# Retention into a snake feed-forward, one core: who transposes q and k of chunks five to eight, and in which slots the later transposes are issued

## The chip, the cores and the metric

The kernel runs on one core of a Trainium2 chip. The metric is the device time of one execution in microseconds (us). The engines are called TensorE (PE in the profile, with PEld for its weight loads), VectorE (DVE), ScalarE (ACT), GpSimd (POOL) and SyncE (SP). SyncE and GpSimd issue the DMA transfers of this kernel.

## What is computed

Two layers in a row. The first is a recurrent retention over 4 batches, 8 heads, 768 positions and head width 64; the second is a feed-forward layer on the 3072 resulting rows of width 512, with a hidden width of 2048 and the activation h + sin(alpha h)^2 / alpha.

```python
for t in range(S):
    state = gamma[None, :, None, None] * state + np.einsum('bhd,bhe->bhde', k[:, :, t], v[:, :, t])
    y[:, :, t] = scale * np.einsum('bhd,bhde->bhe', q[:, :, t], state)
...
h = x @ w_in
s = np.sin(alpha * h)
g = h + s * s / (alpha + 1e-09)
return (g @ w_out).astype(np.float32)
```

## The kernel before

The sequence of each batch is cut into six chunks of 128 positions, 24 chunks in all. The list `order` (also called `P`) first has the first chunk of each of the four batches, then the other five chunks of batch 0, of batch 1, and so on. So P[0] to P[3] are the first chunks, and P[4] to P[8] are the rest of batch 0. The feed-forward layer works on groups of 4, 2, 4, 4, 4, 4 and 2 chunks (`sizes`, L49).

**Loading.** `load_chunk` (L73) brings q, k and v of a chunk by three DMAs from GpSimd's queue, which also change float32 to bfloat16. q and k lie side by side in one tile `qkr`, v in `vr`. GpSimd multiplies v of later chunks by a decay table in place (`scale_v`, L111), between the loads that it issues (L429 to L435); VectorE does it for P[0], P[4] and P[5].

**One chunk of the retention** takes these steps:

- The transposed q and k of all heads are put into `qkT` (128 x 8 x 128, six buffers). There are three ways: `half_T` (L177) for the first three chunks; `stage_T` (L190), eight transposes by TensorE into the PSUM tile `pt` and one copy by VectorE (L197); and `turn` (L199), one DMA from SyncE that transposes from `qkr` into `qkT`.
- `stage_A` (L204): eight matmuls from `qkT` into `pa`, and VectorE's multiplication by the causal mask into `aT` (L214).
- `stage_M` (L233): eight matmuls of the state `s_bd` with `qkT`, eight of `aT` with v, both into `py`; VectorE writes `xT`, the input of the feed-forward layer (L255). It also adds the chunk to the state (`stage_S`, L217), which ScalarE copies to `s_bd` (`keep_S`, L228).

The tiles `pt` of stage_T and `py` of stage_M share one PSUM buffer (tag `ty`).

**The feed-forward layer.** `ff_in(g, f, ...)` makes one of 16 blocks of the hidden layer for a group: four matmuls into `ph` (L270), sine and square on ScalarE (L272, L274), and one VectorE instruction into `gT` (L277). `ff_out` (L284) is one of 16 matmuls that add up one chunk's output in `po` (L287); after the sixteenth, ScalarE copies it to one of three `o_sb` tiles and SyncE stores it. `ph` and `po` share four PSUM buffers.

**The order** is written out by hand; each engine and each queue works through its own instructions in that order. After the first batch of chunks, phase 0 does the rest of group 0's blocks. Then comes a stretch, here called the front (L437 to L451): `outs` is a list of 50 output matmuls of group 0, `fill(n)` issues the next n of them, and between the fills stand the stages of P[4] and P[5]. Phase 1 (L452) does the 16 blocks ("slots") of group 1, P[4] and P[5], whose moving operand has 256 columns, spreads the remaining 19 output matmuls over them, and attaches the stages of P[6] to P[9] to slots through a dictionary. From phase 2 on, slots have 512 columns, and the stages of the next group's chunks and the `turn` of the chunk two further on are attached by a formula (L455 to L470).

Before the change, the DMA transposes of P[4] to P[7] are issued together at L437, ahead of the front; those of P[8] to P[11] in slots 2, 6, 10 and 14 of phase 1.

Of the kernel before, what the change touches and what calls it, by code (L numbers as in the profile page):

```python
# [15 lines left out]
def kernel(  # L16
# [94 lines left out]
    def scale_v(j, eng):  # L111
        eng.tensor_mul(raw["v", j], raw["v", j], kg[:, j % NCH, :, None].to_broadcast([128, H, D]))  # L112
# [77 lines left out]
    def stage_T(j):  # L190
        pt = psum.tile([128, 2 * NP, 128], BF16, name="pt", tag="ty")
        st["qkT", j] = work.tile([128, 2 * NP, 128], BF16, name="qkT", tag="qkT", bufs=6)
        for i in range(2):
            for p in range(NP):
                nc.tensor.transpose(pt[:, i * NP + p, :],
                                    raw["qk"[i], j][:, 2 * p:2 * p + 2, :].rearrange("p h d -> p (h d)"), ident)
        nc.vector.tensor_copy(st["qkT", j], pt)  # L197

    def turn(j):  # L199

        st["qkT", j] = work.tile([128, 2 * NP, 128], BF16, name="qkT", tag="qkT", bufs=6)
        nc.sync.dma_start_transpose(out=st["qkT", j], in_=raw["qk", j].rearrange("p i h d -> p (i h d)"))

    def stage_A(j):  # L204
        qkT = st["qkT", j]
        pa = psum.tile([128, 2, NP, 128], F32, name="pa", tag="pa")
        for p in range(NP):
            for e in range(2):
                r = slice(64 * e, 64 * e + 64)
                nc.tensor.matmul(pa[:, e, p, :], qkT[r, NP + p, :], qkT[r, p, :],  # L210
                                 start=(p == 0), stop=True, skip_group_check=True)
        aT = work.tile([128, 2, NP, 128], BF16, name="aT", tag="aT", bufs=2)
        m = dec.rearrange("p e n t -> p (e n) t") if j % NCH == 0 else mask_bc
        nc.vector.tensor_mul(aT.rearrange("p e n t -> p (e n) t"), pa.rearrange("p e n t -> p (e n) t"), m)  # L214
        st["aT", j] = aT

    def stage_S(j):  # L217
        c = j % NCH
        if c == 0:
            st["ps"] = psum.tile([128, NP, D], F32, name="ps", tag="ps")  # L220
        ps = st["ps"]
        for p in range(NP):
            for e in range(2):
                nc.tensor.matmul(ps[64 * e:64 * e + 64, p, :], raw["k", j][:, 2 * p + e, :], raw["v", j][:, 2 * p + e, :],  # L224
                                 start=(c == 0 and p == 0), stop=True, skip_group_check=True)
        return ps

    def keep_S(j, ps):  # L228
        for e in range(2):
            r = slice(64 * e, 64 * e + 64)  # L230
            nc.scalar.copy(s_bd[(j % NCH + 1) % 2][r, :, r], ps[r, :, :])  # L231

    def stage_M(j):  # L233
        c = j % NCH
        g, i = place[j]
        if g not in xT:
            xT[g] = work.tile([128, KS, sizes[g] * C], BF16, name="xT", tag="xT", bufs=3)
        qkT, aT, vs = st["qkT", j], st["aT", j], raw["v", j]
        py = psum.tile([128, NP, 128], F32, name="py", tag="ty")
        if c > 0:  # L240
            for p in range(NP):
                for e in range(2):
                    r = slice(64 * e, 64 * e + 64)
                    nc.tensor.matmul(py[r, p, :], s_bd[c % 2][:, p, r], qkT[:, p, :],  # L244
                                     start=(p == 0), stop=True, skip_group_check=True)
        for p in range(NP):
            for e in range(2):
                nc.tensor.matmul(py[64 * e:64 * e + 64, p, :], vs[:, 2 * p + e, :], aT[:, e, p, :],  # L248
                                 start=(c == 0 and p == 0), stop=True, skip_group_check=True)
        x = xT[g][:, :, i * C:(i + 1) * C]  # L250
        if c == 0:
            nc.scalar.copy(x, py)
            return
        ps = stage_S(j) if c < NCH - 1 else None
        nc.vector.tensor_mul(x, py, qg[:, c])  # L255
        if ps is not None:
            keep_S(j, ps)
# [42 lines left out]
    def out_pieces(g, tss):  # L300
        return [lambda ts=ts, f=f: ff_out(g, ts, f) for ts in tss for f in range(FF)]
# [55 lines left out]
    def phase(g, outs, att, squares, slots=range(FF)):  # L357

        no, n0, done = len(outs), len(slots), 0
        for n, f in enumerate(slots):  # L360
            add = ff_in(g, f, squares[f % len(squares)])
            for fn in att.get(f, ()):
                fn()
            add()
            while done < no * (n + 1) // n0:
                outs[done]()
                done += 1

    def T(j):
        return lambda: turn(j)  # L370

    def A(j):
        return lambda: stage_A(j)

    def M(j):
        return lambda: stage_M(j)
# [7 lines left out]
    def SK(j):  # L384
        return lambda: keep_S(j, stage_S(j))
# [33 lines left out]
    P = order  # L419
# [4 lines left out]
    def fill(n):  # L424
        for _ in range(n):
            outs.pop(0)()
# [7 lines left out]
        if n in (13, 15, 17):  # L434
            scale_v(order[(n - 11) // 2], nc.gpsimd)  # L435

    for j in P[4:8]:  # L437
        turn(j)
    fill(7)
    scale_v(P[4], nc.vector)  # L440
    fill(5)
    stage_A(P[4])
    keep_S(P[0], stage_S(P[0]))
    fill(5)
    scale_v(P[5], nc.vector)
    fill(5)
    stage_A(P[5])
# [2 lines left out]
    stage_M(P[5])  # L450
    fill(3)  # L451
    phase(1, outs,  # L452
          {1: [A(P[6])], 2: [T(P[8])], 5: [A(P[7]), M(P[6])], 6: [T(P[9])],
           9: [A(P[8]), M(P[7])], 10: [T(P[10])], 13: [A(P[9]), M(P[8]), SK(P[9] - 1)], 14: [T(P[11])], 15: [M(P[9])]}, "A")
    for g in range(2, NG):  # L455
        att = {}
        if g + 1 < NG:
            js = groups[g + 1]
            for i, j in enumerate(js):
                a = i * FF // len(js)  # L460
                n = P.index(j) + 2
                if n < NJ:
                    att.setdefault(a + 2, []).append(T(P[n]))
                att.setdefault(a + 1, []).append(A(j))
                if i > 0:
                    att[a + 1].append(M(js[i - 1]))
                if j % NCH == 1:
                    att[a + 1].append(SK(j - 1))
            att.setdefault(FF - 2, []).append(M(js[-1]))
        phase(g, out_pieces(g - 1, range(sizes[g - 1])), att, "A")  # L470
# [32 lines left out]
```

## Time and profile before

| | us |
|---|---|
| median of three runs (lowest, highest) | 227.9 (227.52, 228.04) |
| the profiled execution | 228.16 |
| its span, first to last instruction | 226.1 |
| TensorE busy | 211.4 |
| ScalarE busy | 164.8 |
| VectorE busy | 130.0 |
| GpSimd busy | 90.3 |

The time of the profiled execution includes 2.06 us outside the span. TensorE is the busiest engine, and busy time is not time at full speed: it counts a matmul at half clock as twice as long. The page's row of the granted clock has 40 slices of 5.65 us. It is at full speed in all but one, the ninth, which begins at 45.2 us. The DMA engines are busy until about 130 us, while the chunks are loaded, and nearly idle after that. The table of DMA issues gives a median of 8.8 us from issue to landing for the 20 transposes, and 9.5 to 10.5 us for the loads of q, k and v.

### The profile page before, as it was taken

Reading aid. Unit: us, or ns where it says so; the run is one execution under the profiler, and the core shown is the slowest. Engines: PE = TensorE matmul, PEld = TensorE weight load, DVE = VectorE, ACT = ScalarE, POOL = GpSimd, SP = SyncE. Lnnn points to the kernel's source line nnn. Section 1 sums busy time; section 2 is a strip of 40 time slices with the busy share of each in tenths; the row PEclk is TensorE's granted clock in tenths of the full one; section 3 lists DMA queues with packets and bytes.
Section 4 is the critical chain, followed back from the end, with each engine's and each line's share of the span. In section 5 each row is a group of like instructions: output and inputs, shape, how many; then the busy total and the mean of one; then the engine's idle time right before and its main releaser. Section 6 shows DMA issues by size and latency. Waiting matters only on the chain.

```text
span 226.1 us, 4226 instructions
## 1 busy us (share of the span) xinstructions
PE 211.4 (93%) x1629; PEld 106.3 (47%) x1629; DVE 130.0 (58%) x214; ACT 164.8 (73%) x322; POOL 90.3 (40%) x105
## 2 busy tenths in 40 slices
PE   7998889579898999999999999999999999999993
PEld 3544433135566454544544544554544454556541
DVE  4777798434787576775645745664753364433300
ACT  7678768223998899978787787687778868777720
POOL 8965346668499788789962000000000000000000
PEclk9999999959999999999999999999999999999999
DMA  9999999999999999999995421431211011111112
GB/s 132 148 185 193 207 204 158 136 152 160 183 183 123 142 172 126 182 156 174 184 169 84 96 65 27 97 96 37 58 46 46 8 42 46 46 49 46 48 60 79
DMA packets 103732, 25.71 MB, mean 114 GB/s; under 512 B 96528, under 2 KB 100640, under 8 KB 103712
## 3 DMA queue, kind: packets, MB, share of 16 engines
q0 software_dynamic: 77024, 13.37, 84.1%
q1 hardware_dynamic: 26688, 12.07, 27.5%
q8 instruction: 12, 0.20, 0.4%
q14 instruction: 8, 0.07, 0.1%
HBM read 27.27 MB, written 6.29 MB: 148 GB/s over the span
## 4 chain that ended last, share of the span: by engine, by line
PE 70%; DMA 15%; POOL 5%; DVE 3%; ACT 3%; issue 2%; POOLq 0%; SPq 0%
PE po L287 34%; PE ph L270 28%; DMA qkr<-in_k_dram 7%; DMA w_in<-in_moe_w_in_dram 4%; DMA qkT<-qkr 4%; PE pa L210 3%; PE py L244 2%; POOL qkr L83 2%; DVE aT L214 2%; PE py L248 2%; ACT s L272 1%; POOL vr L83 1%; PE ps L224 1%; ACT s L274 1%; DVE xT L255 1%
## 5 line engine op out<-in xcount | busy, mean ns | idle before, releaser
L277 DVE SCALAR_TENSOR_TENSOR gT<-s,rec_alpha,ph 128x512 bf16<-128x512 f32 (+3 forms) x118 | 75.7, 645 | 69.8 <-ACT s L274 69.1
L287 PE MATMUL po<-w_out,gT 128*128 128x512 bf16 x384 | 103.6, 386 | 1.9 <-DVE gT L277 1.3
L270 PE MATMUL ph<-xT,w_in 128*128 128x512 bf16 (+3 forms) x472 | 101.5, 339 | 1.3 <-DVE gT L277 0.7
L272 ACT ACTIVATE s<-ph,alpha_sb 128x512 f32<-128x512 f32 (+3 forms) x118 | 71.4, 606 | 31.9 <-PE ph L270 31.8
L270 PEld LDWEIGHTS <-w_in 128*128 128x128 bf16 x472 | 45.3, 98 | 47.5 <-issue 5.0
L274 ACT ACTIVATE s<-s 128x512 f32<-128x512 f32 (+3 forms) x109 | 60.3, 553 | 3.5
L287 PEld LDWEIGHTS <-gT 128*128 128x128 bf16 x384 | 35.9, 99 | 40.0 <-DVE gT L277 4.0
L214 DVE TENSOR_TENSOR aT<-pa,mask 128x1024 bf16<-128x1024 f32 x20 | 24.4, 1221 | 7.8 <-PE pa L210 7.8
L112 POOL TENSOR_TENSOR vr<-vr,kg 128x512 bf16<-128x512 bf16 x21 | 22.1, 1057 | 16.1 <-DMA vr<-in_v_dram 16.1
L83 POOL DMA_DIRECT2D vr<-in_v_dram x24 | 21.8, 906 | 3.2 <-DMA w_in<-in_moe_w_in_dram 1.6
L83 POOL DMA_DIRECT2D qkr<-in_q_dram x23 | 21.3, 925 | 3.8 <-DMA w_in<-in_moe_w_in_dram 1.7
L83 POOL DMA_DIRECT2D qkr<-in_k_dram x23 | 20.4, 888 | 3.8 <-DMA w_out<-in_moe_w_out_dram 3.4
L231 ACT CAST s_bd<-ps 64x256 bf16<-64x256 f32 x40 | 14.4, 361 | 9.1 <-PE ps L224 8.7
L297 ACT COPY o_sb<-po 128x512 f32<-128x512 f32 x23 | 13.2, 574 | 6.9 <-PE po L287 6.9
L255 DVE TENSOR_TENSOR xT<-py,qg 128x512 bf16<-128x512 f32 x20 | 13.7, 683 | 2.3 <-PE py L248 2.2
L210 PE MATMUL pa<-qkT 64*128 64x128 bf16 x192 | 9.7, 222 | 4.4 <-DMA qkT<-qkr 4.2
L309 PE MATMUL spare<-warm 128*128 128x512 bf16 x36 | 12.5, 462 | 1.2 <-DVE warm L131 1.2
L210 PEld LDWEIGHTS <-qkT 64*128 64x128 bf16 x192 | 5.5, 95 | 13.5 <-issue 7.5
L248 PE MATMUL py<-aT,vr 128*64 128x128 bf16 x192 | 9.5, 219 | 0.5 <-DVE rec_alpha L347 0.2
L244 PE MATMUL py<-qkT,s_bd 128*64 128x128 bf16 x160 | 8.3, 225 | 0.2 <-DVE xT L255 0.2
L248 PEld LDWEIGHTS <-vr 128*64 128x64 bf16 x192 | 6.9, 110 | 1.5 <-issue 1.1
L244 PEld LDWEIGHTS <-s_bd 128*64 128x64 bf16 x160 | 5.2, 109 | 4.0 <-issue 1.9
(58 smaller groups left out, 64.0 us busy)
## 6 DMA issues: line engine op xcount, KB each, us to landing
out_dram<-o_sb SPq DMA_DIRECT2D x24, 256.0 KB, 2.3
vr<-in_v_dram POOLq DMA_DIRECT2D x24, 128.0 KB, 10.5
qkr<-in_q_dram POOLq DMA_DIRECT2D x23, 128.0 KB, 9.5
qkr<-in_k_dram POOLq DMA_DIRECT2D x23, 128.0 KB, 10.4
w_in<-in_moe_w_in_dram POOLq DMA_DIRECT2D x4, 512.0 KB, 11.1
w_out<-in_moe_w_out_dram POOLq DMA_DIRECT2D x4, 512.0 KB, 14.9
qkT<-qkr SPq DMA_TRANSPOSE x20, 8.8
q<-in_q_dram SPq DMA_DIRECT2D x1, 256.0 KB, 3.5
```

Source lines behind the costliest of these rows:

```text
L83: nc.gpsimd.dma_start(out=t, in_=chunk_of(src, j))
L112: eng.tensor_mul(raw["v", j], raw["v", j], kg[:, j % NCH, :, None].to_broadcast([128, H, D]))
L210: nc.tensor.matmul(pa[:, e, p, :], qkT[r, NP + p, :], qkT[r, p, :], start=(p == 0), stop=True, skip_group_check=True)
L214: nc.vector.tensor_mul(aT.rearrange("p e n t -> p (e n) t"), pa.rearrange("p e n t -> p (e n) t"), m)
L244: nc.tensor.matmul(py[r, p, :], s_bd[c % 2][:, p, r], qkT[:, p, :], start=(p == 0), stop=True, skip_group_check=True)
L248: nc.tensor.matmul(py[64 * e:64 * e + 64, p, :], vs[:, 2 * p + e, :], aT[:, e, p, :], start=(c == 0 and p == 0), stop=True, skip_group_che ...
L255: nc.vector.tensor_mul(x, py, qg[:, c])
L270: nc.tensor.matmul(ph, w_in[:, i, f * 128:(f + 1) * 128], xT[g][:, i, lo:hi], start=(i == 0), stop=(i == KS - 1))
L272: nc.scalar.activation(out=s, in_=ph, func=ACTF.Sin, scale=alpha_sb[:, f:f + 1])
L274: nc.scalar.activation(out=s, in_=s, func=ACTF.Square)
L277: return lambda: nc.vector.scalar_tensor_tensor(gT[g][:, f, lo:hi], s, rec_alpha[:, f:f + 1], ph, op0=ALU.mult, op1=ALU.add)
L287: nc.tensor.matmul(po[g, ts], gT[g][:, f, ts * C:(ts + 1) * C], w_out[:, f, :], start=(f == 0), stop=(f == FF - 1))
```

## The change

q and k of P[4] to P[7] are transposed by `stage_T` instead of `turn`: for P[4] and P[5] between the fills of the front, for P[6] and P[7] in slots 0 and 3 of phase 1. The DMA transposes of P[8] to P[11] are issued in slots 0, 4, 8 and 12. The other attached stages of phase 1 move too: stage A of P[6] from slot 1 to 2, of P[7] (with stage M of P[6]) from 5 to 6, of P[8] (with stage M of P[7]) from 9 to 10. Slots 13 and 15 and all later phases keep their order.

```diff
     def T(j):
+        return lambda: stage_T(j)
+
+    def X(j):
         return lambda: turn(j)
...
-    for j in P[4:8]:
-        turn(j)
     fill(7)
+    stage_T(P[4])
     scale_v(P[4], nc.vector)
     fill(5)
     stage_A(P[4])
     keep_S(P[0], stage_S(P[0]))
     fill(5)
+    stage_T(P[5])
     scale_v(P[5], nc.vector)
     fill(5)
     stage_A(P[5])
...
     phase(1, outs,
-          {1: [A(P[6])], 2: [T(P[8])], 5: [A(P[7]), M(P[6])], 6: [T(P[9])],
-           9: [A(P[8]), M(P[7])], 10: [T(P[10])], 13: [A(P[9]), M(P[8]), SK(P[9] - 1)], 14: [T(P[11])], 15: [M(P[9])]}, "A")
+          {0: [T(P[6]), X(P[8])], 2: [A(P[6])], 3: [T(P[7])], 4: [X(P[9])], 6: [A(P[7]), M(P[6])], 8: [X(P[10])],
+           10: [A(P[8]), M(P[7])], 12: [X(P[11])], 13: [A(P[9]), M(P[8]), SK(P[9] - 1)], 15: [M(P[9])]}, "A")
...
-                    att.setdefault(a + 2, []).append(T(P[n]))
+                    att.setdefault(a + 2, []).append(X(P[n]))
```

## The prediction

> **What bounds the kernel now.** I read the page first, then the chain of work that ended last, then TensorE's own timeline at the place that the chain names, and last the clock in windows of 1 us. Chunks are named by their place in the kernel's order: P[4] to P[7] are chunks five to eight. "T" is a transpose by TensorE (stage_T), "X" one by the DMA (turn), "A" and "M" are stage_A and stage_M, "SK" is a state update.
>
> The page's first line, and two neighbouring pieces of the chain (start, duration, what):
>
> ```profile
> span 226.1 us, 4226 instructions
> ```
>
> ```profile
> 21.08 16.43 DMA qkr<-in_k_dram
> 37.60 9.12 DMA qkT<-qkr
> ```
>
> P[4]'s k has landed at 37.51, and its X, issued at 37.60, lands at 46.72. TensorE's timeline shows who waits (start, duration, line, instruction, count; in brackets the idle time and what ended it):
>
> ```profile
> 41.98 0.60 PE L287 MATMUL po<-w_out,gT 128*128 128x512 bf16 x2 [0.15 <-DVE gT L277]
> 46.77 0.61 PE L210 MATMUL pa<-qkT 64*128 64x128 bf16 x8 [4.18 <-DMA qkT<-qkr]
> 47.30 0.43 PE L224 MATMUL ps<-vr,kb 128*64 128x64 bf16 x8
> 47.66 4.16 PE L287 MATMUL po<-w_out,gT 128*128 128x512 bf16 x10
> 51.76 0.40 PE L210 MATMUL pa<-qkT 64*128 64x128 bf16 x8
> 52.08 0.41 PE L244 MATMUL py<-qkT,s_bd 128*64 128x128 bf16 x8
> ```
>
> Stage A of P[4] waits 4.18 us for that X, and afterwards ten po matmuls take 4.16 us, over 0.4 us each. The clock says why (window, its length, busy time of PE, PEld, DVE, ACT, POOL; then the granted clock, the DMA share, GB/s):
>
> ```profile
> 43.40:44.40 1.00, 0.00 (x0) 0.00 (x0) 0.00 (x0) 0.00 (x0) 0.07 (x1) 1.00 3.50 120
> 44.40:45.40 1.00, 0.00 (x0) 0.00 (x0) 0.00 (x0) 0.00 (x0) 0.00 (x0) 0.59 3.56 130
> ...
> 50.40:51.40 1.00, 1.00 (x4) 0.30 (x2) 0.00 (x0) 0.59 (x1) 0.00 (x0) 0.50 1.80 157
> 51.40:52.40 1.00, 1.00 (x22) 0.55 (x22) 0.20 (x1) 0.00 (x0) 0.76 (x1) 1.00 2.41 151
> ```
>
> A mean of 0.59 in a window that starts at 1.00 and ends at 0.50 puts the fall near 44.6, some 2.2 us after TensorE ran dry. The clock is back at 51.4. So one late transpose costs twice: the wait, and 4.6 us of matmuls at half speed.
>
> **The change part by part.** The profiled execution took 228.16 us, 2.06 more than its span; the runs' median of 227.9 is 0.26 below it.
>
> *The wait and the slow clock go.* At full speed a 512-column matmul takes 0.216 us (the 41.98 row: 0.60 for two, of which 0.38 is one matmul's own latency). TensorE could issue stage A at 41.98 + 2 x 0.216 = 42.41, and did at 46.77: 4.36 us. From there to 51.76 it needed 4.99 us for eight pa, eight ps and ten po; at full speed 0.32 (51.76 to 52.08), about 0.23 and 2.16, together 2.71. That is 2.28 us more. Gain 6.64.
>
> *What T costs instead.* The first batch's last chunk was transposed by stage_T already:
>
> ```profile
> 18.75 0.40 PE L195 MATMUL pt<-ident,qkr 128*128 128x128 bf16 x4 [0.18 <-DMA qkr<-in_q_dram]
> ...
> 20.01 0.69 DVE L197 COPY qkT<-pt 128x1024 bf16<-128x1024 bf16 x1
> ```
>
> Four transposes take 0.40 us, 0.22 of which is the latency of one, so 0.06 each, and one T of eight is 0.48 us of TensorE and a 0.69 us copy on VectorE. T(P[4]) and T(P[5]) stand in the front, before phase 1: 0.96 us, all on the path, less the 0.15 us wait for gT in the 41.98 row, which they fill: 0.81. Their copies are covered by the five po matmuls (1.08 us) between each T and its stage A, if VectorE is free:
>
> ```profile
> 41.18 0.75 DVE L277 SCALAR_TENSOR_TENSOR gT<-s,rec_alpha,ph 128x512 bf16<-128x512 f32 x1
> ```
>
> VectorE's last gT of phase 0 ends at 41.93, the copy then at 42.62, and TensorE comes to stage A at 42.41 + 0.48 - 0.15 = 42.74. It just fits; without that cover the copy would show up to 0.69 us. Scaling P[4]'s v moves behind the copy on VectorE, and the mask multiply behind that; both lie beside five po matmuls and are not read before stage M of P[4]. Phase 1 thus starts 6.64 - 0.81 = 5.83 us earlier.
>
> T needs raw q and k in time. The k loads of P[6] and P[7], each an issue and then the time to landing:
>
> ```profile
> 35.89 0.88 POOL L83 DMA_DIRECT2D qkr<-in_k_dram  x1 [1.65 <-DMA w_out<-in_moe_w_out_dram]
> qkr<-in_k_dram POOLq DMA_DIRECT2D x1, 128.0 KB, 6.8
> 38.76 0.88 POOL L83 DMA_DIRECT2D qkr<-in_k_dram  x1
> qkr<-in_k_dram POOLq DMA_DIRECT2D x1, 128.0 KB, 10.4
> ```
>
> They land at 42.7 and 49.2 even beside the transposes of before; P[4] and P[5] are earlier in the same queue. TensorE will want P[6] near 50 and P[7] near 53 (phase 1 began with the 55.3 window of before, less 5.8; three slots on). No T waits.
>
> *T(P[6]) and T(P[7]) in phase 1.* Its windows, same columns, and two of VectorE's instructions there:
>
> ```profile
> 55.30:59.60 4.30, 3.65 (x32) 2.32 (x31) 2.64 (x5) 3.73 (x10) 3.71 (x5) 1.00 1.62 226
> 59.60:63.90 4.30, 4.17 (x56) 2.89 (x54) 3.28 (x6) 3.94 (x11) 1.69 (x2) 1.00 1.97 126
> 63.90:68.20 4.30, 4.14 (x56) 2.86 (x55) 3.64 (x7) 4.09 (x12) 4.30 (x6) 1.00 1.74 194
> 68.20:73.80 5.60, 4.88 (x77) 3.29 (x75) 4.21 (x9) 4.67 (x12) 5.60 (x7) 1.00 2.50 121
> 57.19 0.48 DVE L277 SCALAR_TENSOR_TENSOR gT<-s,rec_alpha,ph 128x256 bf16<-128x256 f32 x1 [1.64 <-ACT s L274]
> 57.59 1.22 DVE L214 TENSOR_TENSOR aT<-pa,mask 128x1024 bf16<-128x1024 f32 x1
> ```
>
> TensorE idles 0.65 + 0.13 + 0.16 + 0.72 = 1.66 us there. The two T add 0.96 us; between nothing (they fill idle time) and 0.96 I take 0.5. The two copies bring VectorE in the first four slots to 4 x 0.48 + 1.22 + 2 x 0.69 = 4.5 us, against 4.1 us of TensorE work (four slots of some 0.7, one A of 0.32, two T); the four PSUM buffers of ph carry that lag. Gain so far 5.83 - 0.5 = 5.33.
>
> *The later X must keep up*, for TensorE now comes 5.3 us sooner; A of P[6] to P[8] and the M behind them move back by one slot. Two windows of DMA packets, 100.0 to 101.8 with loads alone, and 42.7 to 55.3 with q0 for loads and q1 for transposes (packets, MB, share):
>
> ```profile
> q0 software_dynamic: 2119, 0.27, 238.3%
> q0 software_dynamic: 8464, 1.07, 163.3%
> q1 hardware_dynamic: 3192, 0.79, 53.0%
> ```
>
> Alone, loads move 2119 / 1.8 = 1177 packets per us, 0.87 us for one load's 1024. In the second window they fill 8464 / 1177 = 7.2 of 12.6 us; 5.4 us are left for 3192 / 1024 = 3.1 transposes, 1.74 us each. The four removed ones stood ahead of every later transfer: 6.9 us of the DMA's time. The X of P[8] and P[9] now, with issue, time to landing, and the stage A that reads each:
>
> ```profile
> 53.94 1.34 SPq L202 DMA_TRANSPOSE qkT<-qkr  x1
> qkT<-qkr SPq DMA_TRANSPOSE x1, 9.5
> 64.89 0.40 PE L210 MATMUL pa<-qkT 64*128 64x128 bf16 x8
> 59.90 2.12 SPq L202 DMA_TRANSPOSE qkT<-qkr  x1
> qkT<-qkr SPq DMA_TRANSPOSE x1, 8.9
> 69.16 0.40 PE L210 MATMUL pa<-qkT 64*128 64x128 bf16 x8
> ```
>
> P[8] lands at 63.4, P[9] at 68.8, only 0.4 us before its use. With 6.9 us less ahead of them they land at 56.5 and 61.9. TensorE comes to P[8] at 64.89 - 5.33 + 0.7 (one slot later) = 60.3, and to P[9] at 69.16 - 5.33 = 63.8: 1.9 us to spare. GpSimd issues these loads, and it can go faster:
>
> ```profile
> POOL vr L112 <- DMA vr<-in_v_dram: 16.1, 11, 3.2
> ```
>
> Its 16.1 us of waits before scaling v are waits for the same DMA and shrink with it. On SyncE the first two output stores no longer stand behind four X; they are issued ahead of X(P[8]) either way. The third store now stands behind X(P[8]), which waits for P[8]'s k; only the next reuse of one of three o_sb buffers waits for that store. No X waits for one of the six qkT buffers: P[10] takes P[4]'s, free since M of P[4].
>
> [...]
>
> After phase 2 TensorE has no gap that this touches. **Sum: 228.16 - 6.64 + 0.81 + 0.5 = 222.8 in the profiled execution, 222.5 at the level of the median.**
>
> **The rivals.** *(a) X(P[9]) comes late.* If a transpose cost the DMA no more than a load, 0.87 us, four free 3.5 us, P[9] lands at 65.3, and TensorE waits 1.5 us: 224.0. [...] For it: the margin of before was 0.4 us. Against it: the packet rates. *(b) VectorE leads in phase 1.* Both copies, 1.4 us, lie on the path beyond the 0.5: 223.9. For it: 4.5 us against 4 in the first slots. Against it: VectorE was idle for at least 15% of each window. *(c) Transposes don't hold the clock up.*
>
> ```profile
> 8.00:36.00 28.00, 25.17 (x192) 12.40 (x193) 22.41 (x41) 21.29 (x45) 14.62 (x19) 1.00 1.55 189
> ```
>
> One more spell at half clock like the one above loses 2.28 us: 224.8. Against it: the clock was 1.00 throughout this stretch, which holds a T. [...] *(d) Slower: the stall moves to P[8].* If the transposes only used DMA time that loads left free, raw k lands no sooner, and X(P[8]) stays at 63.4 while TensorE is there at 60.3. A wait of 3.1 us is past the 2.2 us after which the clock fell, so 2.28 us follow, or twice that if phase 1's short gaps keep the clock down for a second spell: 222.5 + 3.1 + 2.3 to 4.6 = 227.9 to 230.2, 229.1 in the middle. It decides from a landing of X(P[8]) after 62.5. Against it: loads slowed from 1177 to 8464 / 12.6 = 672 packets per us beside transposes.
>
> **How the numbers follow.** Forecast 0.74 at 222.5; (a) 0.11; (b) 0.05; (c) 0.03; (d) 0.07, of it 0.05 slower and 0.02 within 0.2%. I leave 0.01 of the forecast for a tie and 0.01 for slower: faster 0.91, same 0.03, slower 0.06. About 0.2% is what a measurement of this kernel can tell from no change. The range starts at 221.0: T hidden in phase 1 (0.5) and 1.0 of its other idle time gone. It ends at 224.9, above (a), (b) and (c).
>
> **What would show it.** Right: no DMA wait on TensorE before L210, granted clock 1.00 from 40 to 56, the first pa after phase 0 near 42.8, phase 1 near 49.7, X(P[9]) landed by 62. Wrong: an idle TensorE before the pa of P[8] or P[9] ended by a DMA; PEld or PE waiting for the L197 copy; a window below 1.00 in phase 1; loads no denser than 672 packets per us.

## The result, and the profile after

| | before | after |
|---|---|---|
| median of four runs, us (lowest, highest) | 227.72 (227.52, 228.04) | 222.19 (222.06, 222.91) |
| the profiled execution, us | 228.16 | 222.1 |
| its span, us | 226.1 | 220.3 |

The changed kernel takes 0.9762 of the time of before, 95% interval 0.9737 to 0.9787: it is faster by 2.4%. Two later comparisons with other runs of before gave 0.9714 (0.9678 to 0.9749) and 0.9716 (0.9693 to 0.9738). The forecast was 222.5.

The page's row of the granted clock (40 slices of the span, tenths of full speed) no longer has its slow slice:

```profile
PEclk9999999999999999999999999999999999999999
```

TensorE's timeline through the front (start, duration, line, instruction, count; idle time would stand in brackets):

```profile
41.17 0.61 PE L195 MATMUL pt<-ident,qkr 128*128 128x128 bf16 x8
41.62 1.24 PE L287 MATMUL po<-w_out,gT 128*128 128x512 bf16 x5
42.80 0.40 PE L210 MATMUL pa<-qkT 64*128 64x128 bf16 x8
43.12 0.32 PE L224 MATMUL ps<-vr,kb 128*64 128x64 bf16 x8
43.37 1.25 PE L287 MATMUL po<-w_out,gT 128*128 128x512 bf16 x5
44.46 0.61 PE L195 MATMUL pt<-ident,qkr 128*128 128x128 bf16 x8
44.91 1.24 PE L287 MATMUL po<-w_out,gT 128*128 128x512 bf16 x5
46.08 0.40 PE L210 MATMUL pa<-qkT 64*128 64x128 bf16 x8
```

There is no bracket left. Eight transposes take 0.45 us (41.17 to 41.62), five po matmuls 1.09 (43.37 to 44.46), and stage A of P[5] starts at 46.08 where it had started at 51.76.

Phase 1, to within 0.1 us from its first ph to the first of phase 2, of the kernel before and of the changed one (window, length, busy time of PE, PEld, DVE, ACT, POOL; clock, DMA share, GB/s):

```profile
55.50:73.80 18.30, 16.64 (x212) 11.27 (x211) 13.57 (x25) 16.26 (x41) 15.10 (x17) 1.00 2.00 164
```

```profile
49.80:67.80 18.00, 17.50 (x229) 12.08 (x227) 14.82 (x27) 16.36 (x42) 17.50 (x20) 1.00 2.00 156
```

TensorE has 0.86 us more to do, the two T, and yet the stretch is 0.3 us shorter: its idle time fell from 1.66 to 0.50 us. Two waits of TensorE in the kernel before have no counterpart in the changed one:

```profile
59.24 0.38 PE L287 MATMUL po<-w_out,gT 128*128 128x512 bf16 x1 [0.66 <-DVE gT L277]
70.69 0.32 PE L224 MATMUL ps<-vr,qkr 128*64 128x64 bf16 x8 [0.57 <-POOL vr L112]
```

GpSimd, which issues the loads and scales v, is busy for 17.50 of the 18.00 us, up from 15.10 of 18.30.

The DMA transposes of P[8] and P[9] in the changed kernel, each with its issue, its time to landing and the stage A that reads it:

```profile
47.57 1.35 SPq L202 DMA_TRANSPOSE qkT<-qkr  x1
qkT<-qkr SPq DMA_TRANSPOSE x1, 7.4
60.19 0.40 PE L210 MATMUL pa<-qkT 64*128 64x128 bf16 x8
```

```profile
53.89 0.34 SPq L298 DMA_DIRECT2D out_dram<-o_sb  x1
54.41 1.47 SPq L202 DMA_TRANSPOSE qkT<-qkr  x1
qkT<-qkr SPq DMA_TRANSPOSE x1, 7.6
63.87 0.40 PE L210 MATMUL pa<-qkT 64*128 64x128 bf16 x8
```

They land at 55.0 and 62.0, ahead of their uses by 5.2 and 1.9 us. The extra row at 53.89 is the third output store, which stands ahead of P[9]'s transpose in SyncE's queue. In the window 42.7 to 55.3, whose rows of before were 8464 packets of loads and 3192 of SyncE's queue, there are now (q1 also has output stores in both):

```profile
q0 software_dynamic: 11102, 1.40, 180.5%
q1 hardware_dynamic: 1344, 0.79, 30.0%
```

The loads got 31% more through in the same 12.6 us.

### The profile page after: what moved, and what is told of

It is laid out like the page before. It is cut to its first block, busy times and chain, and to the rows that moved or that the text cites. A ratio compares the mean times of both kernels' runs of the same rounds, so it can differ in the third digit from the quotient of the medians.

```text
span 220.3 us, 4282 instructions
## 1 busy us (share of the span) xinstructions
PE 209.3 (95%) x1661; PEld 106.9 (49%) x1661; DVE 132.3 (60%) x218; ACT 164.8 (75%) x322; POOL 90.1 (41%) x105
## 4 chain that ended last, share of the span: by engine, by line
PE 79%; DVE 9%; ACT 6%; DMA 2%; issue 2%; SPq 0%; ACTq 0%
PE po L287 36%; PE ph L270 32%; PE pa L210 3%; DVE aT L214 3%; DVE gT L277 3%; PE py L244 3%; ACT s L272 3%; PE py L248 2%; DMA k<-in_k_dram 2%; ACT s L274 2%; PE spare L309 1%; PE ps L224 1%; DVE s L276 1%; DVE xT L255 1%; PE pt L195 1%
## 5 line engine op out<-in xcount | busy, mean ns | idle before, releaser
L287 PE MATMUL po<-w_out,gT 128*128 128x512 bf16 x384 | 101.9, 380 | 1.3 <-DVE gT L277 0.9
L274 ACT ACTIVATE s<-s 128x512 f32<-128x512 f32 (+3 forms) x109 | 60.3, 553 | 3.5
L255 DVE TENSOR_TENSOR xT<-py,qg 128x512 bf16<-128x512 f32 x20 | 13.7, 684 | 2.3 <-PE py L248 2.2
L309 PE MATMUL spare<-warm 128*128 128x512 bf16 x36 | 11.4, 430 | 1.2 <-DVE warm L131 1.2
```

Of the source, the lines that this page charges most:

```text
L274: nc.scalar.activation(out=s, in_=s, func=ACTF.Square)
L287: nc.tensor.matmul(po[g, ts], gT[g][:, f, ts * C:(ts + 1) * C], w_out[:, f, :], start=(f == 0), stop=(f == FF - 1))
```

## The experiments

The theory was the prediction's account: the late transpose of P[4] costs TensorE its wait and then the half clock; TensorE's own transposes cost little; and taking four transposes off the DMA is what keeps the stall from moving to a later chunk. The main rival grants the first two and says that the DMA had time to spare. All ratios are to the kernel before, run beside the experiment on the same chip; its medians there were 228.3 to 228.5. Where two experiments differ by less than half a percent, their phase 1 in the profile is compared instead.

### The four DMA transposes put back as ballast

```diff
+    old = [near["q"].rearrange("p h d -> p (h d)"), near["k"].rearrange("p h d -> p (h d)"),
+           dec[:, 0].rearrange("p n t -> p (n t)"), dec[:, 1].rearrange("p n t -> p (n t)")]
+    for j, o in zip(P[4:8], old):
+        nc.sync.dma_start_transpose(out=o.bitcast(BF16).rearrange("p (n t) -> p n t", t=128),
+                                    in_=raw["qk", j].rearrange("p i h d -> p (i h d)"))
     fill(7)
     stage_T(P[4])
```

> The changed kernel, with the four DMA transposes of P[4] to P[7] issued as well, into memory that nothing reads. Theory (each transpose takes 1.74 us of the DMA's time from the loads behind it, and taking four away is what lets the later transposes keep up): raw k of P[8] lands near 53.8 as in the kernel before, its DMA transpose near 63.4, TensorE comes to it at 60.2 and waits 3.2 us, the clock falls to half for some 4 us (2 us more): about 227.4. Rival (the transposes used only idle DMA time; the gain is TensorE's own wait and clock alone): the transposes of P[8] and P[9] land by 57 and 63 as in the changed kernel and the time stays at 222.2.

Measured: 231.32 us, 1.0131 (1.0069 to 1.0193) of before: slower than the kernel before by 1.3%. TensorE's timeline at P[8] and P[9], and the clock between them (same columns as above):

```profile
62.41 0.40 PE L210 MATMUL pa<-qkT 64*128 64x128 bf16 x8 [2.23 <-DMA qkT<-qkr]
...
69.91 0.40 PE L210 MATMUL pa<-qkT 64*128 64x128 bf16 x8 [2.46 <-DMA qkT<-qkr]
```

```profile
64.00:66.00 2.00, 2.00 (x9) 1.17 (x8) 1.06 (x3) 1.02 (x3) 2.00 (x4) 0.50 2.06 156
```

The front is as fast as in the changed kernel (phase 1 begins at 49.85), and the stall has moved to P[8], with the half clock behind it. Raw k of P[8] was issued at 41.62 and landed at 53.4, against 41.50 and 47.5 in the changed kernel; its transpose was issued at 53.53, 2.9 us after the two stores ahead of it, so it waited for the data and not for SyncE's queue. The prediction's rival (d) is a real mechanism; what keeps it away is the DMA time that the change frees. The rival of this experiment falls. The size was missed by 4 us: a second wait, of 2.46 us for P[9], and the clock that is low again behind it (0.60 and 0.55 in the windows 70 to 72 and 72 to 74) had been left out of the expectation.

### The wait kept, the clock held up

```diff
     scale_v(P[4], nc.vector)
     fill(5)
+    idle_work(18)
     stage_A(P[4])
```

> The kernel before, with 18 idle 512-column matmuls (3.9 us, their result is not used) on TensorE in the wait for the DMA transpose of P[4], so that only the clock changes. Both theories: granted clock 1.00 from 42 to 52, the ten output matmuls at 0.216 us each, phase 1 begins 2.0 to 2.3 us earlier. Theory (the DMA has no time to spare): the transposes of P[8] and P[9] land at 63.4 and 68.8 as before, TensorE now comes to P[9] 2 us too early, and nearly all is given back: 227.3, 0.3 to 0.5 below before. Rival (the later transposes do not bind): 225.5.

Measured: 227.99 us, 1.0013 (0.9976 to 1.0050): no change. TensorE's timeline of this run, at the wait, behind it, and in phase 1:

```profile
42.29 4.05 PE L309 MATMUL spare<-warm 128*128 128x512 bf16 x18
...
46.84 2.33 PE L287 MATMUL po<-w_out,gT 128*128 128x512 bf16 x10
...
67.47 0.40 PE L210 MATMUL pa<-qkT 64*128 64x128 bf16 x8 [0.43 <-DMA qkT<-qkr]
70.11 0.32 PE L224 MATMUL ps<-vr,qkr 128*64 128x64 bf16 x8 [1.67 <-POOL vr L112]
```

The ten po matmuls took 4.16 us in the kernel before and take 2.33 here, and phase 1 starts at 53.42 instead of 55.60: the second half of the cost was the clock. But of these 2.18 us phase 2 keeps only 0.59 (it starts at 73.33 instead of 73.92): there is a new wait for P[9]'s transpose, and the one for `vr`, a v tile that GpSimd scales, has grown from 0.57 to 1.67 us. Ending the slow clock alone is worth next to nothing while the transfers keep their pace. That the larger part of the loss would come at `vr` was not expected.

### The same wait, filled with transposes

```diff
     fill(5)
+    toss = psum.tile([128, 8, 128], BF16, name="toss", tag="ps")
+    for n in range(72):
+        nc.tensor.transpose(toss[:, n % 8, :], warm[:, :128], ident)
     stage_A(P[4])
```

> The kernel before, with 72 idle 128x128 transposes (some 4 us, their result is not used) on TensorE in the same wait. If transposes by TensorE hold the clock as matmuls do: granted clock 1.00 from 42 to 52, and a time like that of the idle matmuls. [...]

One run, 229.11 us. TensorE's timeline, and the window over the transposes:

```profile
41.84 4.18 PE L444 MATMUL toss<-ident,warm 128*128 128x128 bf16 x72
```

```profile
41.80:46.00 4.20, 4.20 (x75) 4.06 (x75) 0.14 (x1) 0.59 (x1) 1.70 (x3) 1.00 2.40 122
```

72 transposes in 4.2 us, 0.058 each, all at full clock, and phase 1 starts at 53.26, much as with the idle matmuls. Rival (c) falls: in this execution a stretch of nothing but transposes held the clock for 4.2 us, where it had fallen after some 2.2 us of idling. Whether transposes alone would bring a half clock back to full, no run here shows.

The time is longer than with the idle matmuls for another reason, late in phase 1:

```profile
70.44 0.32 PE L224 MATMUL ps<-vr,qkr 128*64 128x64 bf16 x8 [1.86 <-POOL vr L112]
```

```profile
70.00:74.00 4.00, 3.56 (x32) 2.19 (x33) 0.74 (x2) 2.13 (x6) 4.00 (x6) 0.59 2.02 160
```

After a wait of 0.73 us for P[9]'s transpose and this one of 1.86 the clock fell, so the time of this run does not say whether the transposes held the clock; the window over them does.

### Only P[4] by TensorE

```diff
-    for j in P[4:8]:
+    for j in P[5:8]:
         turn(j)
     fill(7)
+    stage_T(P[4])
```

> The kernel before, with P[4] alone transposed by TensorE and P[5] to P[7] still by the DMA ahead of the front. Theory: the wait at 42.4 goes, but the DMA transpose of P[5] lands at 47.7 (49.5 less 1.74) and TensorE is there at 45.6: a wait of 2.1 us, perhaps just too short for the clock to fall; then P[8] and P[9] cost about 1 us each, since only 1.74 us of DMA time was freed: 225.6 (227.7 if the clock falls). Rival (only the first transpose was late, the others do not bind): 221.7 to 222.2.

Measured: 227.63 us, 0.9978 (0.9953 to 1.0004): no change. TensorE's timeline at stage A of P[5], and the clock behind it:

```profile
49.12 0.61 PE L210 MATMUL pa<-qkT 64*128 64x128 bf16 x8 [3.18 <-DMA qkT<-qkr]
```

```profile
50.40:52.40 2.00, 2.00 (x19) 0.98 (x15) 1.19 (x2) 0.73 (x2) 1.33 (x2) 0.50 1.59 173
```

The stall moved by one chunk, and the clock fell again. The transpose of P[5] landed at 49.1, hardly sooner than the 49.5 of before, not at 47.7: the time that one transpose freed went to the loads beside it. From 40.7 to 49.1 they moved 6136 packets where the kernel before moved 4811, and SyncE's queue 1068 where it had moved 2286. By the prediction's own rate of 1177 load packets per us, that is 0.95 us of loads per transpose, an estimate, and not 1.74.

### P[7], or P[6] and P[7], back on the DMA; P[8] on TensorE

Three edits of the front and phase 1. The first diff is for P[7] alone; for both, `turn(P[6])` stands ahead of `turn(P[7])` and T(P[6]) goes from slot 0. The second diff is the opposite step, T(P[8]) in place of its DMA transpose.

```diff
     keep_S(P[0], stage_S(P[0]))
+    turn(P[7])
...
-          {0: [T(P[6]), X(P[8])], 2: [A(P[6])], 3: [T(P[7])], 4: [X(P[9])], 6: [A(P[7]), M(P[6])], 8: [X(P[10])],
+          {0: [T(P[6]), X(P[8])], 2: [A(P[6])], 4: [X(P[9])], 6: [A(P[7]), M(P[6])], 8: [X(P[10])],
```

```diff
-          {0: [T(P[6]), X(P[8])], 2: [A(P[6])], 3: [T(P[7])], 4: [X(P[9])], 6: [A(P[7]), M(P[6])], 8: [X(P[10])],
+          {0: [T(P[6])], 2: [A(P[6])], 3: [T(P[7])], 4: [X(P[9])], 6: [A(P[7]), M(P[6])], 8: [T(P[8]), X(P[10])],
```

> The changed kernel with P[7] transposed by the DMA again, issued in the front behind the state update of P[0]. Theory: its transpose lands by 53 (TensorE wants it at 55.7); TensorE saves one T in phase 1, at most 0.48 us; the 1.74 us of DMA time come back to the transfers behind it, so P[9] lands at 63.7 for a use at 63.4 to 63.9. The two cancel: within 0.4 us of the changed kernel. Rival (T is a plain cost of 0.48 us, the DMA has time to spare): 0.48 us faster.

> The changed kernel with P[6] and P[7] both transposed by the DMA again, issued in the same place. Theory: both land in time (51 and 53 for uses at 52 and 55), but 3.5 us of DMA time come back: P[9] lands at 65.4 for a use at 62.9 to 63.4, a wait of some 2.2 us, 0.5 to 1 us of T saved: 1.2 to 1.7 us slower than the changed kernel, or 3.5 to 4 if the clock falls. Rival (T is a plain cost, the DMA has time to spare): 0.96 us faster.

> The changed kernel with P[8] transposed by TensorE as well, in slot 8 of phase 1. Theory: one T more on TensorE (0.48 us) and on VectorE, 1.74 us of DMA time freed that nothing waits for: 0.2 to 0.5 us slower than the changed kernel, P[9] landing near 60.2. Rival (the loads of v and with them GpSimd's scaling still hold phase 1 up): the same or up to 0.3 us faster.

Measured beside 0.9714 for the changed kernel: P[7] back 0.9726 (0.9687 to 0.9765), P[8] added 0.9735 (0.9704 to 0.9766), both the same as the changed kernel within the noise, which decides neither theory nor rival of these two. P[6] and P[7] back: 0.9987 (0.9958 to 1.0016), the whole gain lost. TensorE's timeline of that run, GpSimd's, and the clock:

```profile
63.92 0.40 PE L210 MATMUL pa<-qkT 64*128 64x128 bf16 x8
...
68.93 0.42 PE L224 MATMUL ps<-vr,qkr 128*64 128x64 bf16 x8 [4.04 <-POOL vr L112]
```

```profile
64.11 1.04 POOL L112 TENSOR_TENSOR vr<-vr,kg 128x512 bf16<-128x512 bf16 x1 [3.72 <-DMA vr<-in_v_dram]
65.10 0.94 POOL L83 DMA_DIRECT2D qkr<-in_q_dram  x1
66.03 0.89 POOL L83 DMA_DIRECT2D qkr<-in_k_dram  x1
66.90 0.90 POOL L83 DMA_DIRECT2D vr<-in_v_dram  x1
67.79 2.08 POOL L112 TENSOR_TENSOR vr<-vr,kg 128x512 bf16<-128x512 bf16 x2
```

```profile
70.00:72.00 2.00, 2.00 (x11) 1.00 (x11) 0.27 (x1) 1.03 (x3) 2.00 (x3) 0.50 1.90 140
```

This was neither the theory nor the rival. The transpose of P[9] came just in time for 63.92 (it landed at 63.9, where 65.4 was expected). What came late was SK in slot 13: it needs v of batch 1's first chunk, which GpSimd scales at L435. That tile was one of the first loads, issued some 60 us before; its scaling only stands in GpSimd's queue behind the scaling of P[10]'s v, and that waited 3.72 us for a late load. With three loads to issue in between, the tile was ready at 68.8, TensorE had waited 4.04 us, and the clock fell.

The landings of P[9] in the other two runs missed as well: 62.1 with P[7] back (63.7 expected), 62.0 with P[8] added (60.2 expected), against 62.0 in the changed kernel. In all of these runs its transpose was issued within 0.6 us behind the third output store. In the run with P[8] added, raw k of P[9] landed at 51.3 and the transpose was issued at 54.32; and GpSimd, at 3.69 us for the three loads and one scaling of a chunk, is busy for all of phase 1 (the last of the four windows below). More free DMA time brought nothing forward there.

### The leftover scaling moved out of the way

To see whether that one wait was the cause, GpSimd scales this tile two chunks earlier, in the kernel with P[6] and P[7] on the DMA and in the kernel before:

```diff
-        if n in (13, 15, 17):
-            scale_v(order[(n - 11) // 2], nc.gpsimd)
+        if n in (11, 15, 17):
+            scale_v(order[max(1, (n - 11) // 2)], nc.gpsimd)
```

> The kernel with P[6] and P[7] by the DMA (x67), in which GpSimd scales the first of the three leftover v tiles two chunks earlier. Theory (what cost 6.7 us there was TensorE's 4 us wait for that tile and the half clock after it; GpSimd had stood behind a late load of v): the wait is gone, the transpose of P[9] comes just in time, that of P[10] some 1.5 us late: 0.5 to 1.5 us slower than the changed kernel. Rival (the DMA is short of time in a way that shows somewhere else as soon as one wait is gone): 3 us or more slower than the changed kernel, with the wait at P[9] or P[10] over 2.2 us and the clock at half again.

> The kernel before with the same earlier scaling. Theory: TensorE's 0.57 us wait for that tile in phase 1 goes and nothing else changes: 0.3 to 0.6 us faster than the kernel before. Rival (the wait is covered by something else that ends at the same time): no change.

Measured, beside 222.10 us and 0.9716 (0.9693 to 0.9738) for the changed kernel: with P[6] and P[7] on the DMA 222.51 us, 0.9739 (0.9717 to 0.9761), where it had been 0.9987. The wait for `vr` was the cause. What is left is 0.47 us in which TensorE waits for P[10]'s transpose (its stage A starts at 70.33), where 1.5 were expected. The kernel before with the same move: 0.9954 (0.9929 to 0.9979), faster by 0.5%, some 1 us where 0.3 to 0.6 were expected; where the rest comes from was not found.

Four kernels now give the price of a T in phase 1, one execution of each. Its window, from its first ph to that of phase 2, with none (P[6] and P[7] on the DMA, scaling moved), one (P[7] on the DMA), two (the changed kernel, run again) and three T (P[8] too):

```profile
49.90:67.50 17.60, 16.64 (x212) 11.21 (x211) 13.76 (x24) 16.07 (x42) 13.69 (x16) 1.00 2.02 173
```

```profile
49.05:66.90 17.85, 16.99 (x220) 11.73 (x219) 14.40 (x25) 16.21 (x42) 17.28 (x20) 1.00 1.91 157
```

```profile
49.15:67.10 17.95, 17.41 (x228) 12.09 (x227) 14.80 (x26) 16.30 (x42) 17.95 (x21) 1.00 2.05 159
```

```profile
49.80:67.95 18.15, 17.84 (x236) 12.60 (x235) 15.34 (x27) 16.42 (x42) 18.15 (x21) 1.00 2.00 140
```

A T adds 0.35 to 0.43 us of TensorE's busy time and 0.10 to 0.25 us of length, 0.18 in the mean; the rest fills waits that the windows with fewer T still have.

Not run, and argued from the order alone: the DMA transposes of P[8] to P[11] put back into slots 2, 6, 10 and 14. Between them SyncE's queue holds only output stores, and none changes its place, so every engine and queue has the same instructions in the same order as in the changed kernel. So their new slots are no part of the gain. The moves of stage A by one slot were not run by themselves either; the next section has what the runs show of them. No kernel was measured to be faster than the changed one.

## Why the prediction was right

Its mechanism held: the wait and the slow clock went, four transposes off the DMA kept the stall from coming back, and T was cheap. Of its terms one was mis-sized, in sign too, and one of its landings came out right by luck.

- **Wait and slow clock, 6.64 us less 0.81 for two T: 5.83.** Phase 1's first ph moved from 55.60 to 49.92, 5.68 us. The changed kernel's execution was 0.16 us behind before the edit already (the po at 35.73 stands at 35.89 there), so the term is 5.84. The run with the clock held up gives its clock part by itself: from stage A of P[4] to that of P[5] it took 3.30 us (46.27 to 49.57), 2.90 without a new wait of 0.40 at P[5], where the kernel before took 4.99. That is 2.09 us for the 2.28 forecast.
- **The copy just fits.** Stage A of P[4] was forecast for 42.74 and starts at 42.80.
- **T(P[6]) and T(P[7]) cost 0.5 us of phase 1.** This is the term that was mis-sized: from first ph to first ph, phase 1 went from 18.32 (55.60 to 73.92) to 17.95 us (49.92 to 67.87). The two T cost 0.35 us by the four windows; against that, idle time of before went. The prediction counted such idle time only as a place to hide T. The 0.57 us of TensorE's wait for the scaled `vr` of before went because GpSimd waited less for loads; moving that scaling in the kernel before showed that it was worth something by itself. The 0.66 us wait for gT at 59.24 stands at the same place in all four experiments built on the kernel before, which have stage A of P[6] in slot 1, and in none built on the changed one, which have it in slot 2. It fits the move of that stage, to which the prediction gave no gain; no run moves the stage alone. So the total gain at the start of phase 2 was 6.05 us instead of 5.33, and the profiled execution, 222.10, lies 0.7 us below the 222.8 of the sum, the median of 222.19 0.3 below its 222.5.
- **The later X keep up.** P[8] and P[9] were forecast to land at 56.5 and 61.9 for uses at 60.3 and 63.8. They landed at 55.0 and 62.0 for 60.2 and 63.9. The ballast run shows that the freed DMA time is what did it. The size is another matter. P[8] gained 8.4 us, not 6.9. That P[9] came within 0.1 is luck: its raw k landed at 51.2 (issued at 45.63, 5.6 us), but its transpose was issued at 54.41, behind the third store, which waits for ScalarE's copy of a chunk that TensorE finishes in slot 2. In the kernel before that store (59.40) stood in front as well. So 5.5 of the 6.8 us came from TensorE's own earlier progress and 1.3 from a shorter way to landing. The prediction saw the third store behind X(P[8]) and not X(P[9]) behind the third store. Its 1.74 us per transpose missed the landings of P[5] and P[9] in four experiments by 1.4 to 1.8 us; no run confirms it.

What the prediction missed is the nearest danger. It took the transpose of P[9], with 1.9 us to spare, for the tightest place, and dismissed GpSimd in a sentence, because its waits for v shrink with the loads. The runs show that they shrink only as long as the loads come in time, and that one tile at the end of GpSimd's queue breaks first: two transposes put back onto the DMA cost 6 us there and nothing at P[9]. Both kernels' own profiles point at it, the 0.57 us wait of before, and in the changed kernel the row of the scaling (the tile is the first of the two, ready near 63.2) and the row that reads it:

```profile
62.14 2.08 POOL L112 TENSOR_TENSOR vr<-vr,kg 128x512 bf16<-128x512 bf16 x2
64.66 0.29 PE L224 MATMUL ps<-vr,qkr 128*64 128x64 bf16 x8
```

That is some 1.5 us to spare, less than P[9]'s 1.9. Rival (d) had the right mechanism, a stall that moves to a later chunk. The ballast run shows the slower kernel it spoke of, by 1.3%.

So four transposes by TensorE, at 0.45 us of its time each, do two things: two of them (P[4], P[5]) remove the stall, and the other two (P[6], P[7]) pay for the loads behind them. Without the second pair the stall comes back at another place, unless the scaling is moved as well.

## What to carry to other kernels

When a stall is removed, everything behind it is wanted sooner by as much: for each later transfer, and for each engine that follows a transfer in order, subtract the gain from the time to spare before counting it. Price a DMA transfer by what it takes from the transfers queued beside it, not by its latency: a transpose here took a median of 8.8 us from issue to landing and, by the estimate from the run with P[4] alone by TensorE, 0.95 us of loads. A piece of work whose input has long been there should not stand in a queue behind one that waits for a load: with P[6] and P[7] on the DMA, moving one such scaling forward took the time from 0.9987 to 0.9739 of before.

## What the runs showed of the hardware that was not expected

- **Waits of 1.86, 2.23 and 4.18 us were followed by the half clock, in two of these three executions only after work had resumed.** In the ballast run TensorE waited 2.23 us and went on at 62.41. The window 62 to 64 has a mean of 0.89, so the fall came near 63.6, 3.4 us after the wait began and 1.2 us after it ended. In the kernel before, with the wait of 4.18, it fell some 2.2 us after TensorE ran dry. In the run with idle transposes it fell at 70.7, 2.1 us after the wait of 1.86 began and 0.3 after it ended at 70.44; a wait of 0.73 us had preceded it a little earlier. In the run with idle matmuls a wait of 1.67 us after one of 0.43 left the clock at 1.00 over the whole span. So two nearly equal waits, 1.67 and 1.86, came out differently, and which length is safe these runs do not say.
- **The spells at half clock listed here had two lengths, 3.4 and 6.8 us.** By the means of the windows the clock was low for 3.4 us in the run with idle transposes (70.7 to 74.1) and the first time in the ballast run (63.6 to 67.0, a mean of 0.75 from 66 to 68), and 6.8 in the kernel before (44.6 to 51.4) and with P[6] and P[7] on the DMA (68.0 to 74.8).
- **In two executions a transpose overtook a load that had been issued before it.** With P[6] and P[7] on the DMA, v of P[10] was issued at 50.73 and took 13.3 us, the DMA transpose of P[9] was issued at 54.30 and took 9.6: it landed at 63.9, the load at 64.0. In the kernel before the lead is larger: v of P[9], issued at 48.41, took 13.7 us and landed at 62.1; the transpose of P[7], issued at 49.27, took 7.7 and landed at 57.0. Issue and time to landing of the first pair, the load first:

```profile
50.73 0.90 POOL L83 DMA_DIRECT2D vr<-in_v_dram  x1
vr<-in_v_dram POOLq DMA_DIRECT2D x1, 128.0 KB, 13.3
54.30 3.30 SPq L202 DMA_TRANSPOSE qkT<-qkr  x1
qkT<-qkr SPq DMA_TRANSPOSE x1, 9.6
```
